# Four pieces of a weight load: cut across the columns instead of across the partitions

## The chip, the core and the metric

The kernel runs on one core of a Trainium2 chip. The metric is device time in microseconds (us): the median of three runs of the whole program, one launch. The core has five engines with a program each: TensorE (PE, matrix products, with its weight loads as PEld), VectorE (DVE), ScalarE (ACT), GpSimd (POOL) and SyncE (SP). Transfers between the chip's main memory (HBM) and the core's memory (SBUF, 128 partitions) are issued by SP, ACT or POOL and carried out by 16 DMA engines. A transfer is taken apart into packets, here one for each contiguous run of bytes, a row of a partition.

## What is computed

Attention with 4 batches, 12 heads, 448 positions and 64 channels, whose heads are mixed before and after the softmax, and behind it a gated feed-forward layer:

```python
scores = scale * np.matmul(q, k.transpose(0, 1, 3, 2))
scores = np.einsum('bhij,hg->bgij', scores, w_pre)
attn = np.exp(scores - np.max(scores, axis=-1, keepdims=True))
attn = attn / (np.sum(attn, axis=-1, keepdims=True) + 1e-09)
attn = np.einsum('bhij,hg->bgij', attn, w_post)
x = np.matmul(attn, v)                # to (1792, 768)
gate = 1.0 / (1.0 + np.exp(-(x @ w_gate)))
out = (gate * (x @ w_val)) @ w_out    # 768 -> 1536 -> 768
```

## The kernel before

**The attention** runs to about 350 us of the profile. The queries of a batch are cut into blocks of up to 120, a block into sets of ten, and two sets make a unit; there are 92 units. The main loop has a slot for each unit and does in slot s the parts of several units: `regroup` of unit s+5, `premix` and `rowmax` of unit s+2, `expo` of the same, `norm`, `scale` and `p_lo` of unit s+1, `postmix` and `mix` of unit s, and parts of the scores of a coming block and of the weighted sum `av` of the last one.

The scores lie in SBUF tiles named st with the queries on the partitions. Mixing heads needs them with heads and queries on the partitions, so `regroup` (L206; L208 for a lone set) moves them with two transfers a unit from st into one of four tiles T, 120 rows of 1792 bytes each, from SBUF to SBUF. `premix` (L216) reads T with eight matmuls. T is issued in slot s for slot s+3 where `premix` reads it. Its buffer is one of four, and becomes free with the `premix` of four units earlier.

**The queue around the change.** SP issues nearly every transfer of this part, in program order: the T of each slot, k of the next batch (L137, 128 rows of 1792 bytes), v (L171, 128 rows of 4096 bytes), q (L145), the stores xs of the attention's result (L274, rows of up to 480 bytes), and the pieces of the weights that this change touches (L1005).

**The weights.** They come as 64-bit floats and are turned into 32-bit ones on the chip. A weight tile has 128 partitions and 768 numbers, so 6144 bytes a partition. It is read from the fourth byte on (`[:, 3:]`), 6141 bytes a row, so that the words come to lie as the conversion wants them. Most tiles are loaded with one transfer of 128 rows (L1035, after the attention). The first eight are taken during the attention by `early(k, step)`, tile k from slot 6+7k on: steps 0 to 3 in slots 0, 1, 2 and 3 of the tile load a piece each (L1005); step 4, in slot 8, is POOL's first pass (`top`, L1041), which reads one byte of each of the 768 words of all partitions; further passes of POOL follow in slots 9 and 10; steps 7 and 8 (slots 11 and 12) convert half of the columns each on DVE (L1059); steps 9 and 10 take the sums of the two halves on ACT (L981); step 11 (slot 14) stores the tile (L1063). Three buffers named raws are used in turn.

The order of the instructions on every engine is that of the program; no scheduler moves them. The feed-forward layer behind the attention follows a plan that is made before the launch from costs and due times; the change touches none of them.

Of the kernel before, what the change touches and what calls it, by code (L numbers as in the profile page):

```python
# [15 lines left out]
I8 = mybir.dt.int8  # L16
# [452 lines left out]
class _Moe:  # L469
# [530 lines left out]
    def early(self, k, step):  # L1000

        raw = self.free["R"][k % len(self.free["R"])]
        if step < 4:
            rows = slice(32 * step, 32 * step + 32)
            self.nc.sync.dma_start(out=raw.bitcast(I8)[rows, :8 * self.WE - 3], in_=self.src[k].bitcast(I8)[rows, 3:])  # L1005
            return
        names = ("raw", k), ("half", k)
        self.at.update({names[0]: raw, names[1]: self.free["H"][0]})
        if step < 7:
            self.top(k, step - 4, self.nc.gpsimd)  # L1010
        elif step < 9:
            self.convert(names[0], k, step - 7)
        elif step < 11:
            self.sum_of(names[0], ("w", k // 4), k % 4, step - 9, self.at[names[1]].bitcast(F16))
        else:
            self.keep_w(names[0], k, self.nc.sync)
        for name in names:
            del self.at[name]
# [241 lines left out]
```

## Time and profile before

| | |
|---|---|
| median of 3 runs | 824.03 us (817.82 to 831.54) |
| the profiled execution | 823.65 us, of which the span of the trace is 821.8 us |
| busy: PE, DVE, ACT, POOL | 778.4, 648.9, 550.8, 276.5 us |
| weight pieces (L1005) | 32 transfers, 191.9 KB each |
| transfers into T (L206, L208) | 176 of 210.0 KB, 8 of 105.0 KB |

A busy engine in such a profile is not an engine at its peak: the ends of pipelined matmuls are modelled. The chain is read backwards from the end of the program or of a stretch: at each step it names what released the step that came last. The DMA share of a stretch is the mean busy share of the 16 DMA engines. q1 is the queue of SP's and ACT's transfers. A packet of a few bytes stands at the end of each engine's part of a transfer.

### The profile page before, as it was taken

What the parts mean: (1) busy time and instruction counts of PE and PEld (TensorE: products, weight loads), DVE (VectorE), ACT (ScalarE), POOL (GpSimd) and SP (SyncE); (2) the same over time, 40 slices, a digit from 0 to 9 for tenths busy, and PEclk for the clock granted to TensorE, in tenths of its full rate; (3) what the DMA queues carried; (4) which work ended last, traced back from release to release, by engine and by line L of the source; (5) the groups of instructions that cost most, each with busy time, mean ns of one, the idle gap of its engine ahead of it and who ended that gap; (6) DMA issues with size and microseconds to landing.
All of it is one profiled execution on the core that took longest, in us unless ns stands there. A gap on an engine that the chain in (4) does not pass through costs nothing.

```text
span 821.8 us, 23240 instructions
## 1 busy us (share of the span) xinstructions
PE 778.4 (95%) x9530; PEld 424.1 (52%) x9530; DVE 648.9 (79%) x1105; ACT 550.8 (67%) x1058; POOL 276.5 (34%) x438
## 2 busy tenths in 40 slices
PE   8889998999999999978999999999997999999998
PEld 2445555564644655654555555555553455455554
DVE  4979998898978989988998989679772998998000
ACT  3867887787767887868776867668762785653100
POOL 1535666555654644420122232224220312110000
PEclk9999999999999999979999999999999999999999
DMA  5787568868886575694725554755568789996001
GB/s 187 224 212 228 174 214 238 237 196 179 225 253 201 178 219 166 221 167 149 243 91 146 171 205 188 250 192 198 189 201 140 266 304 262 409 350 274 34 34 67
DMA packets 78690, 166.13 MB, mean 202 GB/s; under 512 B 20984, under 2 KB 54104, under 8 KB 78584
## 3 DMA queue, kind: packets, MB, share of 16 engines
q1 hardware_dynamic: 70920, 136.03, 55.3%
q0 software_dynamic: 7088, 28.13, 9.1%
q8 instruction: 74, 1.21, 0.6%
q10 hardware_dynamic: 576, 0.51, 0.2%
q14 instruction: 32, 0.26, 0.1%
HBM read 87.77 MB, written 38.15 MB: 153 GB/s over the span
## 4 chain that ended last, share of the span: by engine, by line
PE 63%; DMA 17%; ACT 6%; DVE 6%; issue 4%; POOL 2%; SPq 0%; ACTq 0%; POOLq 0%; DVEq 0%
PE bank L1114 27%; PE bank L1125 14%; PE pm L216 6%; PE av L285 6%; DMA T<-st 6%; PE qk L158 5%; PE mx L258 4%; DMA xs<-xt 3%; ACT e L228 3%; DMA k<-in_kp_dram 2%; DVE m L1098 2%; DVE nm L221 2%; DMA max_out<-one_out 2%; DMA m<-max_out 1%; ACT mix L266 1%
## 5 line engine op out<-in xcount | busy, mean ns | idle before, releaser
L1114 PEld LDWEIGHTS <-m 128*128 128x128 f16 x1512 | 148.3, 98 | 151.5 <-issue 10.9
L1114 PE MATMUL bank<-m,m 128*128 128x448 f16 x1116 | 216.1, 354 | 10.2 <-DVE m L1141 5.7
L228 ACT ACTIVATE e<-pm,nm 128x448 f32<-128x448 f32 x180 | 114.9, 639 | 66.2 <-DVE nm L221 58.9
L240 POOL TENSOR_SCALAR ph<-e,ss 128x448 f16<-128x448 f32 x180 | 112.7, 638 | 57.7 <-DVE ss L234 36.7
L221 DVE TENSOR_REDUCE nm<-pm 128x1 f32<-128x448 f32 x180 | 103.5, 615 | 30.4 <-PE pm L216 29.3
L246 DVE SCALAR_TENSOR_TENSOR pl<-e,ss,ph 128x448 f16<-128x448 f32 x180 | 121.8, 716 | 1.2 <-POOL ph L240 1.2
L1125 PEld LDWEIGHTS <-m 128*128 128x128 f16 x756 | 73.9, 98 | 69.9 <-DMA m<-w 1.1
L216 PE MATMUL pm<-T,w 64*64 64x448 f32 (+1 forms) x720 | 103.9, 567 | 2.9 <-DMA T<-st 2.2
L258 PEld LDWEIGHTS <-ph 64*128 64x128 f16 x2880 | 69.0, 95 | 71.6 <-issue 39.6
L266 ACT ACTIVATE mix<-mx 128x960 f32<-128x960 f32 (+1 forms) x92 | 102.8, 1117 | 4.0 <-PE mx L258 3.9
L285 PE MATMUL av<-mix,v 128*64 128x120 f32 (+1 forms) x1504 | 95.5, 271 | 9.9 <-issue 7.6
L158 PE MATMUL qk<-k,q 64*64 64x448 f32 (+2 forms) x640 | 98.4, 555 | 2.7 <-ACT st L164 2.7
L1125 PE MATMUL bank<-m,m 128*128 128x448 f16 x468 | 93.1, 352 | 0.6 <-DMA m<-w 0.6
L285 PEld LDWEIGHTS av<-mix,v 128*64 128x64 f32 x1504 | 75.3, 139 | 17.8 <-issue 10.6
L258 PE MATMUL mx<-w2hi,ph 64*128 64x60 f16 x1440 | 72.6, 190 | 9.0 <-ACT mix L266 8.4
L1114 PE MATMUL bank<-m 128*128 128x448 f16 x396 | 79.1, 356 | 0.0
L1049 POOL CAST raws<-raws 128x768 f16<-128x768 bf16 x36 | 37.6, 1045 | 122.7 <-ACT raws L1043 122.6
L258 PE MATMUL mx<-w2lo,ph 64*128 64x60 f16 x1440 | 72.3, 189 | 1.7 <-issue 1.7
L258 PE MATMUL mx<-w2hi,pl 64*128 64x60 f16 x1440 | 72.3, 189 | 0.0
L233 POOL TENSOR_SCALAR ss<-ss 128x2 f32<-128x2 f32 (+1 forms) x92 | 31.2, 339 | 118.7 <-ACT e L228 117.5
L1141 DVE TENSOR_TENSOR m<-bank,m 128x448 f32<-128x448 f32 x72 | 44.6, 620 | 24.5 <-PE bank L1114 16.7
L258 PEld LDWEIGHTS <-pl 64*128 64x128 f16 x1440 | 63.0, 95 | 0.0
(119 smaller groups left out, 1064.7 us busy)
## 6 DMA issues: line engine op xcount, KB each, us to landing
T<-st SPq DMA_DIRECT2D x176, 210.0 KB
m<-w SPq DMA_DIRECT2D x60, 384.0 KB
raws<-in_w_dram SPq DMA_DIRECT2D x28, 767.6 KB
hs<-m POOLq DMA_DIRECT2D x48, 224.0 KB, 4.8
m<-hs SPq DMA_DIRECT2D x15, 672.0 KB
w<-m POOLq DMA_DIRECT2D x21, 384.0 KB, 4.8
v<-in_vb_dram SPq DMA_DIRECT2D x12, 512.0 KB
raws<-in_w_dram SPq DMA_DIRECT2D x32, 191.9 KB
```

What stands on the lines that cost most here:

```text
L158: nc.tensor.matmul(sc[e][s0:s1, :S], lhsT=q[rows, c, s0:s1], rhs=k[rows, :], start=True, stop=True)
L216: nc.tensor.matmul(pm[bank][64 * x:64 * x + 64, :S], lhsT=w1[rows], rhs=T[rows, x], start=True, stop=True)
L221: nc.vector.tensor_reduce(nm[:, i:i + 1], pm[bank][:, :S], axis=AX.X, op=ALU.max, negate=True)
L228: nc.scalar.activation(out=e_t[u][:, i], in_=pm[units[u][2][i]][:, :S], func=AF.Exp, bias=nm_t[u][:, i:i + 1], scale=1.0, accum_out=ss_t[u ...
L240: nc.gpsimd.tensor_scalar(ph[:, i], e_t[u][:, i], ss_t[u][:, i:i + 1], 1.0, op0=ALU.mult, op1=ALU.mult)
L246: nc.vector.scalar_tensor_tensor(pl[:, i], e_t[u][:, i], ss_t[u][:, i:i + 1], p_t[u][0][:, i], op0=ALU.mult, op1=ALU.subtract)
L258: nc.tensor.matmul(mx[:, x, i, jb * HK:(jb + 1) * HK], lhsT=p[rows, i, JB[jb]:JB[jb] + 128], rhs=w[rows], start=(k == 0), stop=(k == 2))
L266: nc.scalar.activation(out=out.rearrange("p g (y r) -> p y g r", r=HALF), in_=mx_t.pop(u), func=AF.Copy, scale=1.0 / (P_UP * W_UP))
L285: nc.tensor.matmul(av_t[bi][64 * i:64 * i + 64, c % 4, :n], lhsT=vt[b, u][:, h + i, jb, :], rhs=mixes[bi % 2][:, jb, 2 * c + i, :n], start ...
L1114: self.nc.tensor.matmul(self.f32(bank), lhsT=w[a][:, k], rhs=x[b][:, k], start=self.START[i] and k == r == 0, stop=k == self.KH - 1 and r ...
L1125: self.nc.tensor.matmul(self.f32(bank), lhsT=w[a][:, k], rhs=b[bb], start=self.START[i] and j == k == r == 0, stop=j == OUT_TILES - 1 and ...
L1141: self.nc.vector.tensor_tensor(self.f32(out), self.f32(bank), self.f32(snap), op=ALU.add)
```

## The change

Each tile is still loaded in four pieces, in the same slots and by the same engine. A piece was a quarter of the partitions (32 rows, 6141 bytes each). It is now a quarter of the columns: 128 rows of 1536 bytes, in the last piece 1533. `self.WE` is 768, and `2 * self.WE` bytes are 192 of the 64-bit numbers.

```diff
         raw = self.free["R"][k % len(self.free["R"])]
         if step < 4:
-            rows = slice(32 * step, 32 * step + 32)
-            self.nc.sync.dma_start(out=raw.bitcast(I8)[rows, :8 * self.WE - 3], in_=self.src[k].bitcast(I8)[rows, 3:])
+            b, e = 2 * self.WE * step, min(2 * self.WE * (step + 1), 8 * self.WE - 3)
+            self.nc.sync.dma_start(out=raw.bitcast(I8)[:, b:e], in_=self.src[k].bitcast(I8)[:, b + 3:e + 3])
             return
```

On SP, the first tile's pieces stand like this between the transfers of k, q and T (T_170 to T_173 are the four T buffers; in brackets the semaphores that an instruction waits for):

```order
 L137 DMA k<-in_kp_dram 128x448 [waits DMAHW1_49]
-L1005 DMA raws<-in_w_dram 32x6141 [waits DMAHW2_49]
+L1005 DMA raws<-in_w_dram 128x1536 [waits DMAHW2_49]
 L206 DMA T_170<-st 120x1x448 [waits DMAHW3_49,DVE_49,Activation_49]
 L206 DMA T_170<-st 120x1x448 [waits DMAHW4_49,PE_49]
 L137 DMA k<-in_kp_dram 128x448 [waits DMAHW5_49]
-L1005 DMA raws<-in_w_dram 32x6141 [waits DMAHW6_49]
+L1005 DMA raws<-in_w_dram 128x1536 [waits DMAHW6_49]
 L206 DMA T_171<-st 120x1x448 [waits DMAHW7_49,PE_49]
 L206 DMA T_171<-st 120x1x448 [waits DMAHW0_49,PE_49]
```

No row has moved, and the pieces wait for the same semaphores; only their shape differs.

On DVE, in the middle of the attention, the first of a tile's two half-width conversions (L1059) stands among the work of a slot:

```order
 L164 COPY st<-qk 120x448 [waits PE_49]
 L246 SCALAR_TENSOR_TENSOR pl<-e,ss,ph 128x448 [waits Pool_49] x2
-L1059 SCALAR_TENSOR_TENSOR raws<-raws 128x384 [waits DMAHW7_49,DMAHW6_49,DMAHW2_49]
+L1059 SCALAR_TENSOR_TENSOR raws<-raws 128x384 [waits DMAHW6_49,DMAHW2_49]
 L234 RECIPROCAL ss<-ss 128x2 [waits Pool_49]
 L221 TENSOR_REDUCE nm<-pm_116 128x1 [waits PE_49]
```

It keeps its place and names the pieces that hold its own half of the columns, where it named pieces of all partitions; with some tiles the second conversion and ACT's sums (L981) name the rest.

## Rows read from the trace of the kernel before

**Rows 1.** The profile's page, part 4: the chain's shares by engine.
```profile
PE 63%; DMA 17%; ACT 6%; DVE 6%; issue 4%; POOL 2%; SPq 0%; ACTq 0%; POOLq 0%; DVEq 0%
```

**Rows 2.** The chain of 40 to 256 us: shares, then start, length and what.
```profile
by line: DMA T<-st 20.1%; PE pm L216 13.5%; PE av L285 13.2%; PE qk L158 9.2%; DMA xs<-xt 8.6%; PE mx L258 8.4%; DMA k<-in_kp_dram 5.0%; ACT e L228 3.7%; issue 3.5%; DVE nm L221 2.8%; ACT mix L266 2.1%; DVE pl L246 2.0%; ACT st L164 1.8%; P
...
52.16 8.87 DMA T<-st
...
219.19 9.07 DMA T<-st
228.33 7.67 DMA T<-st
...
245.40 7.35 DMA T<-st
```

**Rows 3.** The chain of 255 to 346 us: its shares.
```profile
by line: PE pm L216 22.4%; PE av L285 22.3%; PE mx L258 18.3%; PE qk L158 17.1%; ACT e L228 4.4%; ACT mix L266 3.4%; DMA T<-st 3.2%; issue 2.7%; DVE nm L221 2.6%; DVE pl L246 1.4%; ACT st L164 0.5%; DVE one_w L994 0.4%; DVE vm L176 0.4%; DV
```

**Rows 4.** Stretches, L216 alone: us, PE, PEld, clock, DMA share, GB/s.
```profile
43.00:65.00 22.00, 5.50 (x40) 1.04 (x40) 0.92 0.85 212
215.00:240.00 25.00, 8.81 (x46) 2.18 (x44) 1.00 0.88 228
255.00:280.00 25.00, 6.97 (x56) 1.54 (x60) 1.00 0.60 196
```

**Rows 5.** Instructions of the tiles raws: ns min/median/max, first and last start.
```profile
L1005 SPq DMA_DIRECT2D raws<-in_w_dram x32: 322/494/1441, 43.2 to 251.3; - x32
L1035 SPq DMA_DIRECT2D raws<-in_w_dram x28: 327/328/1026, 384.4 to 585.6; - x28
...
L1041 POOL TENSOR_SCALAR raws<-raws x16: 2172/2204/2223, 76.9 to 275.6; 128x768 int16<-128x768 int8 x8, 128x768 int32<-128x768 int16 x8
```

**Rows 6.** Who waited for L1005: engine, tile, line, us and times.
```profile
  PEld pm L216: 0.3, 2
```

**Rows 7.** SP's timeline in two places: start, length, line, transfer, count.
```profile
110.58 0.50 SPq L1005 DMA_DIRECT2D raws<-in_w_dram  x1
111.19 3.40 SPq L206 DMA_DIRECT2D T<-st  x4
114.69 0.45 SPq L171 DMA_DIRECT2D v<-in_vb_dram  x1
115.24 1.67 SPq L206 DMA_DIRECT2D T<-st  x2
...
220.01 0.50 SPq L1005 DMA_DIRECT2D raws<-in_w_dram  x1
...
238.89 0.33 SPq L1005 DMA_DIRECT2D raws<-in_w_dram  x1
```

**Rows 8.** Transfers of 554.5 to 556.5 us: packets, then q1's packets, MB, share.
```profile
DMA packets 149, 0.82 MB, mean 408 GB/s; under 512 B 16, under 2 KB 16, under 8 KB 149
...
q1 hardware_dynamic: 149, 0.82, 98.6%
```

**Rows 9.** The same of 87.8 to 89.4 us.
```profile
DMA packets 86, 0.25 MB, mean 153 GB/s; under 512 B 22, under 2 KB 56, under 8 KB 86
...
q1 hardware_dynamic: 86, 0.25, 53.6%
```

**Rows 10.** The same of 335 to 337 us.
```profile
DMA packets 301, 0.49 MB, mean 245 GB/s; under 512 B 28, under 2 KB 301, under 8 KB 301
...
q1 hardware_dynamic: 301, 0.49, 64.5%
```

**Rows 11.** The same of 84 to 86 us.
```profile
DMA packets 515, 0.24 MB, mean 121 GB/s; under 512 B 515, under 2 KB 515, under 8 KB 515
...
q1 hardware_dynamic: 515, 0.24, 41.7%
```

**Rows 12.** The same of 233.5 to 235.5 us.
```profile
DMA packets 282, 0.46 MB, mean 232 GB/s; under 512 B 23, under 2 KB 282, under 8 KB 282
...
q1 hardware_dynamic: 282, 0.46, 82.1%
```

## The prediction

> **What bounds the kernel now.** I read four views, from the whole to the single transfer. The chain of the whole program first [rows 1]: TensorE holds 63% of it and transfers 17%, so a transfer can set the time, if it is in the right stretch. The 32 pieces are issued between 43.2 and 251.3 us [rows 5], so only that stretch can answer directly. The chain of 40 to 256 us [rows 2] is quite another than that of 255 to 346 us [rows 3], where the same attention runs without pieces. In the first, transfers into T hold 20.1%, xs 8.6% and k 5.0%, together 33.7% of 216 us, or 73 us; in the second, T holds 3.2%. The legs are long: a T that is issued at 219.19 us releases its reader only after 9.07 us.
>
> The stretches [rows 4] say the same. In 215 to 240 us TensorE does 46 matmuls of L216 in 25 us; at eight to a slot that is 5.75 slots, 4.35 us each. In 255 to 280 us it is 56, or 3.57 us. The busy share of the 16 DMA engines is 0.88 in the slow stretch and 0.60 in the fast one, with the granted clock at 1.00 in both. So in part of the stretch the DMA engines are the bound, and what a piece costs them counts there. Elsewhere a piece is beside the path.
>
> **What a piece's own reader sees.** The four pieces of a tile are issued in slots 0 to 3 and POOL first reads the tile in slot 8; the first piece goes out at 43.2 us and the first L1041 runs at 76.9 us [rows 5]. The last piece has five slots, over 17 us at 3.57 us a slot, and the longest transfer leg of the chain that stands here is 9.07 us [rows 2]. Nobody waits for a piece but a weight load of L216, 0.3 us in two waits [rows 6]. The new form keeps that: POOL's first pass reads a byte of every word in all columns and needs all four pieces, as before. The waits that the change puts on the half-width DVE conversions and ACT sums name pieces that landed before POOL's pass began, so they cost nothing. If that cover went, POOL's pass would wait for a landing, and the tile's store behind it.
>
> **What the change adds and removes, step by step.** SP issues the same 32 instructions in the same places. Each goes from 32 rows of 6141 bytes to 128 rows of 1536 (1533 in the last of four), so the bytes are the same.
>
> *Issue on SP: 0.* A 32-row piece takes 494 ns in the median, 322 at the least; a whole tile with 128 rows (L1035) takes 328, 327 at the least [rows 5]. What follows is no slower behind many rows: two T take 1.67 us behind the 128 rows of v at 114.69 us, and four take 3.40 us behind a 32-row piece at 110.58 us, so 0.84 and 0.85 us each [rows 7].
>
> *Time on the DMA engines.* I work in rows, with the busy share times 16 engines times the window, over the rows in it. A piece has 32 rows, 32 pieces have 1024: 64 per engine, if they spread evenly.
> - An old row, cheapest: 554.5 to 556.5 us holds next to nothing but rows of a whole tile, same length, all 128 partitions: 98.6% of 32 engine-us over 133 rows, less the 16 small packets, is 236 ns [rows 8].
> - An old row as a piece: 87.8 to 89.4 us holds 30 long rows, 34 of T (86 packets, 22 under 512 bytes, 56 under 2 KB) and 22 small ones. 53.6% of 25.6 engine-us is 13.72; less 34 at 75 ns and 22 at no more than 26 ns leaves 10.6, or 353 ns [rows 9]. So a row costs half as much again when all 16 engines write into 32 partitions.
> - A new row is not in the trace. A row of 1792 bytes takes 75 ns where T is alone (64.5% of 32 us over 273) [rows 10], one of 480 takes 26 (41.7% of 32 us over 515) [rows 11]; on the line between them 1536 bytes take 65. Beside k loads, in the slow stretch, a row of 1792 takes 100 (82.1% of 32 us over 259, less the small ones) [rows 12]; by its length a new row would take 86.
> - So four new rows take 260 (alone), 344 (by length, beside others) or 400 ns (each as dear as the 1792) against 236 to 353. I set 344 against 353: both are prices of a busy stretch, and the piece is of the old form. The difference is -9 ns per old row; the ends are 260-353 = -93 and 400-236 = +164 ns.
>
> *What of it is on the path.* I counted in SP's order: 13 of the 32 pieces are issued inside a transfer leg of the chain or up to 2.5 us ahead of one; two rows per engine each. That is 26 rows: -0.2 us, with ends of -2.4 and +4.3. With all 64 rows on the path it is -0.6, with ends of -6.0 and +10.5.
>
> The sum: 823.65 us for the profiled execution, -0.2, is 823.45 us; I say 823.5. The median of the runs is 824.03, from 817.82 to 831.54, so this one is a usual one, and the runs scatter more than the sum moves.
>
> [...] The old piece shows 353 ns for a row that costs 236 over all partitions [rows 8, 9]. [...] The new row starts 3 bytes past its grid in HBM as the old one did, but four times as often. [...]
>
> **The rivals.**
> *Faster, the old pieces held up T.* Long rows that meet in 32 partitions keep their engines and the T rows behind them. For it: legs of 7 to 9 us in the stretch with pieces and 3.2% after it [rows 2, 3], and 353 against 236 ns. The chain has 20.1% of 216 us, 43 us, in T. Half of that excess gone would be about 18 us, 805 to 806. A more modest form, a fifth of T's legs gone, is 8.7 us: 815. Against it: the leg that starts at 228.33 us lasts 7.67 us, and SP issues no piece between 220.01 and 238.89 us [rows 2, 7]. What fills the engines there is k, and the slow slots go on without a piece.
>
> *Slower, four rows for one fill engines that are full.* This is one mechanism: at a DMA share of 0.88, each new row at 100 ns against an old one at 236 delays the T behind it, all 64 rows count, and 10.5 us makes 834. It decides where T, issued three slots before its use, lands later than that use; in the slow stretch that point is reached already [rows 2, 4]. Past 2% it would take 16.5 us, so 257 ns more per old row, a new row at 123 ns or over from 236, dearer than any 1792 row read here. [...] Against it: the old pieces already cost 353.
>
> *The change moves bytes that are hidden anyway.* Where no transfer is on the chain (19 pieces), nothing changes. This is the same result as the forecast, by another way: 823.65.
>
> **How the numbers follow.** The forecast with the hidden rival, a move of under 2.4 us down or 4.3 up: 0.66, and 823.5. Faster by 3 to 16 us by the T legs: 0.14; by more: 0.06. Slower by 5 to 16 us: 0.10; by more: 0.04. The range takes the bounds of all 64 rows, 823.65-6.0 and +10.5, hence 817.7 to 834.2; at the low end I go on to 815 for the fifth of T's legs, and the scatter of the runs (817.82 to 831.54) lies inside: 815 to 834. The forecast's own range is 821 to 828. Two per cent, 16.5 us, is about what a measurement of this kernel can tell from no change. Faster by more than that 0.06, within it 0.90, slower by more 0.04.
>
> **What would show it right or wrong.** Right: L1005 with 32 issues near 0.33 to 0.5 us; about 3,000 more packets on q1, most of 1536 bytes, at the same bytes; T still near a fifth of the chain of 40 to 256 us; the slots of 215 to 240 us still over 4 us. The row price is wrong if a stretch with pieces shows a DMA share that is 0.03 higher or lower at the same work. The cover is wrong if anyone on POOL, DVE or ACT waits for raws<-in_w_dram. The forecast is wrong if T's share of that chain falls under a tenth (then the first rival), or if waits of L216 for T rise by several us in stretches that had none, 65 to 115 us above all (then the second).

## The result and the profile after

The changed kernel takes 814.07 us in the median against 823.88 us of the kernel before, 20 runs of each, so 9.8 us less. Without the slow runs of either kernel the ratio is 0.9907, with a 95% interval of 0.9879 to 0.9934; it is that of the two means, which lie 7.7 us apart. The move is under 2%, but clear of the scatter, and 8 to 10 us by either measure. The forecast of 823.5 us, with a range of its own of 821 to 828, was wrong. The median lies 0.9 us under the low end of the wide range; 824.03 us times the ratio, 816.4 us, lies just inside it.

The profiled execution took 810.96 us (span 809.2), 3.1 us less than the median: the two traces differ by 12.7 us, the kernels by less. The chain of the whole program after the change, by engine, against [rows 1]:

```profile
PE 73%; DMA 9%; ACT 7%; DVE 6%; issue 2%; POOL 2%; SPq 0%; ACTq 0%; DVEq 0%; POOLq 0%
```

Transfers fell from 17% to 9%. All of it happened beside the attention. The last matmul of L216 stands at 356.5 us in the trace before and at 344.0 us in the one after (first the line of before, then that of after, from the list of instructions that read T, whose columns are ns min/median/max, first and last start):

```profile
L216 PE MATMUL pm<-T,w x720: 533/587/951, 17.4 to 356.5; 64*64 64x448 f32 x176, 60*64 60x448 f32 x4
...
L216 PE MATMUL pm<-T,w x720: 533/536/587, 16.6 to 344.0; 64*64 64x448 f32 x175, 60*64 60x448 f32 x5
```

That is 12.5 of the 12.7 us between the two profiled executions. Of these, 1.7 us stand already at the first piece (43.2 us before, 41.5 after), where nothing differs yet. The chain of 40 to 256 us after the change, as in [rows 2] (shares by line, then start, length and what):

```profile
by line: PE av L285 18.0%; PE pm L216 17.4%; PE qk L158 13.5%; PE mx L258 12.0%; DMA T<-st 8.2%; DMA xs<-xt 5.5%; ACT e L228 4.8%; ACT mix L266 3.1%; DVE nm L221 2.9%; issue 2.8%; POOL raws L1041 2.7%; ACT st L164 2.2%; DVE pl L246 2.1%; PO
...
189.71 7.71 DMA T<-st
218.42 8.71 DMA T<-st
```

T fell from 20.1% to 8.2% of it. The leg between two loads of k, with no piece ahead of it, is still there: 7.67 us at 228.33 before, 8.71 at 218.42 after. Those of 8.87, 9.07 and 7.35 us at 52, 219 and 245 us, all near a piece, are gone, and with them the longest T of the chain before, which [rows 2] leave out, 10.46 us at 135.92; a new one of 7.71 stands at 189.71 us.

The stretches of [rows 4] show the same by slots (us, PE, PEld, clock, DMA share, GB/s, of L216 alone; the first line is of before, the others of after):

```profile
115.00:140.00 25.00, 5.89 (x48) 1.25 (x48) 0.93 0.82 232
...
43.00:65.00 22.00, 6.01 (x52) 1.36 (x56) 1.00 0.87 245
115.00:140.00 25.00, 6.61 (x56) 1.25 (x48) 1.00 0.77 236
215.00:240.00 25.00, 8.91 (x48) 1.97 (x48) 1.00 0.88 250
```

43 to 65 us has 52 matmuls where there were 40, and moves 245 GB/s where it moved 212, at much the same busy share (0.87 and 0.85). 115 to 140 us has 56 where there were 48. In 215 to 240 us little has changed: 48 against 46.

What the DMA engines did is best read over the same work, from the first piece to 10 us past the last. The first two rows are of the kernel before, 43.2 to 261.3 us, the others of the changed one, 41.5 to 249.9 us (packets, then q1's packets, MB and share of 16 engines):

```profile
DMA packets 29267, 47.02 MB, mean 216 GB/s; under 512 B 9766, under 2 KB 25301, under 8 KB 29221
...
q1 hardware_dynamic: 29221, 46.35, 76.2%
```

```profile
DMA packets 32336, 47.07 MB, mean 226 GB/s; under 512 B 9766, under 2 KB 29373, under 8 KB 32289
...
q1 hardware_dynamic: 32289, 46.40, 75.3%
```

The bytes are the same and the packets 3068 more, but 76.2% of 218.1 us is 166.2 us on each engine, and 75.3% of 208.4 us is 156.9: 9.3 us less. Taken packet by packet from the same stretches of the two traces, it is not the pieces that became cheaper:

| packets of q1 | mean ns before | after | us on each engine before | after |
|---|---|---|---|---|
| the pieces (per old row: 1 long, then 4 short) | 349 | 4 x 91.2 = 365 | 22.3 | 23.3 |
| 1792 bytes (T and k) | 97.4 | 92.5 | 93.0 | 88.1 |
| 4 bytes (the end of a transfer on an engine) | 24.4 | 10.4 | 4.2 | 1.8 |
| 2880 bytes (q) | 180.2 | 163.7 | 11.3 | 10.3 |
| 4096 bytes (v) | 255.6 | 231.4 | 13.8 | 12.9 |

The pieces cost 1.0 us more; everything else costs some 10 us less. The rows of 1792 bytes that were in flight together with a row of a piece took 104.5 ns in the mean before and 94.0 after; the others took 93.0 and 91.4. So most of what they gained was gained beside a piece. The 4-byte packets are another matter, of which the last section tells.

### The profile page after: what moved, and what is told of

It is laid out like the page before. It is cut to its first block, busy times and chain, and to the rows that moved or that the text cites. A ratio compares the mean times of both kernels' runs of the same rounds, so it can differ in the third digit from the quotient of the medians.

```text
span 809.2 us, 23239 instructions
## 1 busy us (share of the span) xinstructions
PE 770.3 (95%) x9530; PEld 419.5 (52%) x9530; DVE 649.6 (80%) x1105; ACT 550.5 (68%) x1058; POOL 276.3 (34%) x438
## 4 chain that ended last, share of the span: by engine, by line
PE 73%; DMA 9%; ACT 7%; DVE 6%; issue 2%; POOL 2%; SPq 0%; ACTq 0%; DVEq 0%; POOLq 0%
PE bank L1114 29%; PE bank L1125 18%; PE av L285 7%; PE pm L216 7%; PE qk L158 6%; PE mx L258 5%; ACT e L228 3%; DMA T<-st 3%; DMA xs<-xt 2%; DVE nm L221 2%; DMA max_out<-one_out 2%; DVE m L1098 1%; ACT mix L266 1%; DMA m<-max_out 1%; DMA max_x<-vr 1%
## 5 line engine op out<-in xcount | busy, mean ns | idle before, releaser
L258 PEld LDWEIGHTS <-ph 64*128 64x128 f16 x2880 | 66.8, 93 | 70.8 <-issue 37.8
L216 PE MATMUL pm<-T,w 64*64 64x448 f32 (+1 forms) x720 | 100.2, 561 | 2.1 <-DMA T<-st 1.4
L158 PE MATMUL qk<-k,q 64*64 64x448 f32 (+2 forms) x640 | 95.6, 545 | 3.9 <-ACT st L164 3.9
L285 PE MATMUL av<-mix,v 128*64 128x120 f32 (+1 forms) x1504 | 93.3, 268 | 5.2 <-ACT xt L293 3.4
L258 PE MATMUL mx<-w2hi,ph 64*128 64x60 f16 x1440 | 70.6, 188 | 10.5 <-ACT mix L266 9.1
L285 PEld LDWEIGHTS av<-mix,v 128*64 128x64 f32 x1504 | 73.9, 138 | 12.5 <-ACT xt L293 4.3
L258 PE MATMUL mx<-w2lo,ph 64*128 64x60 f16 x1440 | 70.3, 187 | 1.2 <-issue 1.2
L258 PE MATMUL mx<-w2hi,pl 64*128 64x60 f16 x1440 | 70.3, 187 | 0.0
L233 POOL TENSOR_SCALAR ss<-ss 128x2 f32<-128x2 f32 (+1 forms) x92 | 30.0, 326 | 105.6 <-ACT e L228 104.3
L258 PEld LDWEIGHTS <-pl 64*128 64x128 f16 x1440 | 61.3, 93 | 0.0
```

What stands on the lines that cost most here:

```text
L158: nc.tensor.matmul(sc[e][s0:s1, :S], lhsT=q[rows, c, s0:s1], rhs=k[rows, :], start=True, stop=True)
L216: nc.tensor.matmul(pm[bank][64 * x:64 * x + 64, :S], lhsT=w1[rows], rhs=T[rows, x], start=True, stop=True)
L258: nc.tensor.matmul(mx[:, x, i, jb * HK:(jb + 1) * HK], lhsT=p[rows, i, JB[jb]:JB[jb] + 128], rhs=w[rows], start=(k == 0), stop=(k == 2))
L285: nc.tensor.matmul(av_t[bi][64 * i:64 * i + 64, c % 4, :n], lhsT=vt[b, u][:, h + i, jb, :], rhs=mixes[bi % 2][:, jb, 2 * c + i, :n], start ...
```

## The experiments

Two theories at first. **P**: what matters is which partitions a piece writes. **R**: what matters is how long its rows are, because short ones let other rows in between. Each ratio below is to runs of the kernel before on the same chip.

### Which partitions, or which length

The two parts of the change, one at a time: 32 rows of 6141 bytes in every fourth partition, and 32 neighbouring partitions with rows of 1533 bytes.

```diff
-            rows = slice(32 * step, 32 * step + 32)
+            rows = slice(step, 128, 4)
```

> A piece keeps its 32 rows of 6141 bytes, but takes every fourth partition instead of 32 neighbours. Theory P (which partitions a piece writes decides: rows that land in 32 neighbouring partitions collide with each other and hold the other transfers' rows behind them) expects what the changed kernel gives, a ratio of about 0.99 to the kernel before (some 814 us) and long rows near 240 to 290 ns in the mean instead of 349. Theory R (the length of a row decides: short rows let T's rows and TensorE's instruction loads in between) expects no change, 1.00 (824 us), and T's rows as dear as before (mean 91 ns).

Measured: 1.0512 (1.0466 to 1.0558), 865.42 us. Neither theory had that.

```diff
+            rows, n = slice(32 * step, 32 * step + 32), 2 * self.WE
+            out, src = (t.bitcast(I8)[rows].rearrange("p (c n) -> p c n", n=n) for t in (raw, self.src[k]))
+            self.nc.sync.dma_start(out=out[:, :, :n - 3], in_=src[:, :, 3:])
```

> A piece keeps its 32 neighbouring partitions, but each partition's row is cut into four rows of 1533 bytes (three bytes between them that nothing reads are left out). Theory P expects no gain, 1.00 (824 us) or a little above, since there are 98,000 more bytes' worth of row starts on crowded partitions, and rows well over 95 ns in the mean. Theory R expects the changed kernel's gain, 0.99 (814 us).

Measured: 0.9991 (0.9965 to 1.0018), 821.79 us. (The 98,000 bytes in that text are a slip: it is 3072 more rows.) Rows as short as the changed kernel's, in the old partitions, gain nothing. R falls. The mean of the short rows is 96.3 ns in the trace, near the changed kernel's 91.2, and the rows of 1792 bytes stay at 98.8 (104.8 beside a piece).

The two with 64 partitions and half the columns, neighbours and every second one:

```diff
+            rows, b = slice(64 * (step // 2), 64 * (step // 2) + 64), 4 * self.WE * (step % 2)
+            e = min(b + 4 * self.WE, 8 * self.WE - 3)
+            self.nc.sync.dma_start(out=raw.bitcast(I8)[rows, b:e], in_=self.src[k].bitcast(I8)[rows, b + 3:e + 3])
```

> A piece has 64 neighbouring partitions (0 to 63 or 64 to 127) and half the columns, rows of 3072 bytes. [...] Theory R expects half of the gain, 0.995, and the same as for every second partition.

Measured: 0.9985 (0.9955 to 1.0015), 821.39 us. Twice the partitions and half the row length give nothing that can be measured.

The other takes `rows = slice(step // 2, 128, 2)`, with the rest as in the last diff.

> As the kernel with 64 neighbouring partitions and rows of 3072 bytes, but a piece takes every second partition, so 64 partitions over the whole range. Theory P expects the whole gain, 0.99 (814 us). Theory R expects 0.995, and no difference to the 64 neighbouring partitions.

Measured: 1.0478 (1.0443 to 1.0513), 862.99 us.

Why both strided ones are slow, the waits of SP's own queue show, in 40 to 256 us of the first of them (engine, line, waited for, us, times, longest):

```profile
SPq L1005 <- POOL ss L233: 40.4, 15, 5.8
SPq L1005 <- DMA w<-raws: 21.4, 5, 5.7
```

There is no such row before. The three buffers lie side by side in one tile. It looks as if a slice with a stride over the partitions is taken as a range that reaches over the other buffers too: a piece waits for POOL and for the store of another tile, and every T behind it on SP waits as well. With these waits in them, the two runs say nothing of partitions.

### The same without those waits

The buffers as tiles of their own, first for the strided pieces, then for the pieces before, as a control:

```diff
-        raws = top.tile([128, 13 * H * D // 2], F32, name="raws")
+        raws = [top.tile([128, n * H * D // 2], F32, name=f"raws{i}") for i, n in enumerate((4, 4, 4, 1))]
...
```

> Every fourth partition again, 32 rows of 6141 bytes, but with the three buffers as tiles of their own, so that a piece does not wait for POOL's passes over a tile in another buffer (SP's waits are then those of the kernel before). [...] If striding itself is dear, it stays slow, 1.03 to 1.05. If only the number of partitions of a piece counts, 1.00.

Measured: 0.9902 (0.9866 to 0.9938), 814.23 us.

> The control for that: the kernel before, pieces of 32 neighbouring partitions, with the three buffers as tiles of their own. All theories expect 1.00 (0.997 to 1.003); what it differs by is to be taken off the strided one.

Measured: 0.9977 (0.9944 to 1.0010), 820.79 us. So the old long rows, 32 to a piece, give the changed kernel's time if the 32 partitions lie apart: 6.6 us between the two medians, with no overlap of the intervals. The length of a row and the number of partitions are the same in both. That the 5% of every fourth partition were the waits is shown as well: no piece waits for POOL any more. Every second partition was not tried again. The price of a long row that theory P named for every fourth partition, 240 to 290 ns, was missed: it is 337 in the mean, against 359 in the control. It is again the others that gained more, the rows of 1792 bytes beside a piece with 95.2 ns against 107.3.

### Which 64 partitions, or too few of them

The pair that tells these apart, with `slice(32, 96)` here and `slice(0, 64)` in the other:

```diff
+            to = self.free["R"][(k + step // 2) % len(self.free["R"])]
+            rows, b = slice(32, 32 + 64), 4 * self.WE * (step % 2)
+            e = min(b + 4 * self.WE, 8 * self.WE - 3)
+            self.nc.sync.dma_start(out=to.bitcast(I8)[rows, b:e], in_=self.src[k].bitcast(I8)[rows, b + 3:e + 3])
...
+        nc.gpsimd.memset(raws, 0.0)
```

Both kernels leave out half of each tile, which stays zero, so that they move as many bytes as the kernel before.

> A pair with the next kernel, alike but for the partitions. Every piece writes rows of 3072 bytes into partitions 32 to 95, the first two of a tile into its own buffer, the other two into the buffer of the next tile (which overwrites them), so the bytes stay those of the kernel before, but half of each tile is never loaded (zeros, from one memset of POOL at the start). [...] Theory N (only the number of partitions of a piece counts, and 64 are still too few) expects what 64 neighbours gave before, 0.9985, and the same in both kernels.

Measured: 0.9887 (0.9837 to 0.9938), 812.80 us.

> The other of the pair: partitions 0 to 63 in every piece, all else as in the one with 32 to 95, and half of each tile never loaded as there. [...] Number of partitions: equal to its pair.

Measured: 1.0002 (0.9968 to 1.0036), 822.36 us. The two differ in one number and by 9.6 us: the whole gain. Neither the length of a row, nor the count of partitions, nor a stride is different. So theory N, with equal times for the pair, falls. What in the path of a transfer sets 0 to 63 apart from 32 to 95, no trace here shows. The traces do speak against one reading, that pieces of 0 to 63 are carried by fewer DMA engines: both kernels wrote 2729 packets of 4 bytes, one for each engine's part of a transfer, in the stretches below. The transfers over the same work, of the kernel with 0 to 63 (43.3 to 262.0 us) and then of the one with 32 to 95 (41.6 to 248.7 us):

```profile
DMA packets 30364, 47.20 MB, mean 216 GB/s; under 512 B 9769, under 2 KB 25349, under 8 KB 30317
...
q1 hardware_dynamic: 30317, 46.53, 77.5%
```

```profile
DMA packets 30331, 47.17 MB, mean 228 GB/s; under 512 B 9769, under 2 KB 25298, under 8 KB 30284
...
q1 hardware_dynamic: 30284, 46.50, 74.9%
```

The same bytes take 169.5 us of each engine (77.5% of 218.7) and 155.1 us (74.9% of 207.1). Worked out in the same way from their traces, each from its first piece to 10 us past the last, the kernels whose pieces keep their four slots and bring no new waits fall into two groups, and the times go with them:

| pieces | us on each engine | ratio |
|---|---|---|
| 32 neighbours, long rows (before) | 166.2 | 1 |
| 32 neighbours, tiles of their own | 167.0 | 0.9977 |
| 32 neighbours, short rows | 165.8 | 0.9991 |
| 64 neighbours, halves | 168.3 | 0.9985 |
| 0 to 63 | 169.5 | 1.0002 |
| 32 to 95 | 155.1 | 0.9887 |
| every fourth, long rows, tiles of their own | 157.1 | 0.9902 |
| all 128, short rows (the change) | 156.9 | 0.9907 |
| all 128, short rows, tiles of their own | 157.3 | 0.9870 |

### How finely to cut

All over the 128 partitions: a tile in one transfer in slot 0, in two in slots 0 and 2, and in eight of 768 bytes a row in slots 0 to 7 (the last as an edit of the changed kernel).

```diff
+            if step == 0:
+                self.nc.sync.dma_start(out=raw.bitcast(I8)[:, :8 * self.WE - 3], in_=self.src[k].bitcast(I8)[:, 3:])
             return
```

> Each tile in one transfer of 128 rows of 6141 bytes, in slot 0; nothing in slots 1 to 3. If only the partitions that a transfer covers matter, the gain stays, 0.99, perhaps 0.985, since 24 transfers fewer are issued and a long row is cheaper by the byte (236 ns against four times 65). If the cutting into pieces also matters (a whole tile is 8 rows of 236 ns ahead of the next T on each engine, near 2 us), T comes late in that slot: 0.995 to 1.00.

Measured: 0.9927 (0.9889 to 0.9964), 816.09 us.

```diff
+            if step % 2 == 0:
+                b, e = 2 * self.WE * step, min(2 * self.WE * (step + 2), 8 * self.WE - 3)
```

> Each tile in two transfers over all partitions, 128 rows of 3072 bytes, in slots 0 and 2. Partitions alone: 0.99. Cutting matters: between the four pieces (0.99) and the whole tile.

Measured: 0.9931 (0.9899 to 0.9963), 817.69 us. One, two or four transfers cannot be told apart.

```diff
+            j = step if step >= 0 else 3 - step
+            b, e = self.WE * j, min(self.WE * (j + 1), 8 * self.WE - 3)
...
+        for step in range(-4, 0):
+            at(6 + 7 * k + 3 - step, moe.early, k, step)
```

> Each tile in eight transfers over all partitions, 128 rows of 768 bytes, in slots 0 to 7. Row starts are then 8 per old row; a row of 768 bytes costs some 37 ns alone (on the line between 480 and 1792 bytes), so 298 ns per old row against 260 for four, 2.4 us more over all on each engine, and 32 more transfers on SP at 0.33 to 0.5 us. Partitions alone: 0.99 to 0.995. If finer pieces let more through: under 0.99.

Measured: 1.0220 (1.0161 to 1.0278), 838.77 us, against all that was expected. T does not come later: the weight loads of L216 wait 0.9 us for it in 40 to 260 us, 8.2 before. But the eighth piece goes out in slot 7 and POOL reads the tile in slot 8. DVE's wait behind POOL and POOL's own, in 40 to 260 us (`top` is L1044 in this kernel, `norm` L233; the last line is of the kernel before):

```profile
DVE ss L234 <- POOL ss L233: 31.7, 13, 7.0
...
POOL raws L1044 <- DMA xs<-xt: 11.9, 3, 5.7
POOL raws L1044 <- DMA T<-st: 11.7, 2, 5.9
...
DVE ss L234 <- POOL ss L233: 5.3, 9, 1.2
```

Before, POOL's pass waited for no transfer. The profile names a piece for 2.4 us of the pass's waits, and xs and T for the rest; that these too are waits for the late piece is likely, since the pass reads neither, and not shown. `norm` stands behind `top` on POOL, and the softmax waits for `norm`. That run took the cover away that the prediction had put at five slots, and it costs more than the change gave. Eight pieces that end in time were not tried.

### Both together

> The changed kernel (four pieces over all partitions, rows of 1536 bytes) with the three buffers as tiles of their own. [...] If short rows cost anything that counts, it is slower than the strided pieces by 2 us or more.

Measured: 0.9870 (0.9832 to 0.9909), 813.94 us, beside 823.86 us before on that chip. It is level with the changed kernel's 0.9907 and with the strided 0.9902, within their intervals. Nothing here beats the changed kernel by a margin that can be measured.

## Why the prediction was wrong, step by step

**The bound: right.** Transfers set the time in part of the stretch, and the gain came in that part.

**The reader's slack: right.** The longest transfer leg of the chain was 10.79 us (a k at 41.31 us), not 9.07, still well under 17. After the change only weight loads of L216 wait for a piece (0.5 us, three times), as before, and the row of L1005 has the same median, 496 ns against the 494 of [rows 5]:

```profile
L1005 SPq DMA_DIRECT2D raws<-in_w_dram x32: 328/496/1462, 41.5 to 239.9; - x32
...
  PEld pm L216: 0.5, 3
```

The kernel with eight pieces, where one slot of slack is left, took 2.2% longer.

**The price of a row: right.** A piece's row was set at 353 ns from [rows 9]; all 1024 have 349 in the mean. A new row alone was put at 65 by the line between two lengths. In 106.4 to 107.2 us of the trace after, nearly nothing but new rows runs (116 of 1533 bytes, and nine of T), and it says so:

```profile
DMA packets 151, 0.19 MB, mean 243 GB/s; under 512 B 26, under 2 KB 151, under 8 KB 151
...
q1 hardware_dynamic: 151, 0.19, 67.9%
```

67.9% of 12.8 engine-us over 125 rows is 69.5 ns with the 26 small packets in it, and 64 if those are taken at 26 ns. In the busy stretch four rows cost 365 where 344 were set. So the term is +1.0 us for all 64 old rows of an engine instead of -0.6: a small miss. In 41.5 to 249.9 us of the trace after, the 3072 rows of 1536 bytes and the 1024 of 1533 both take 65 ns in the median and 62 at the least.

**What of it is on the path: the step that failed.** It counted the pieces' own rows and nothing else: 13 of 32 pieces, -0.2 us. The pieces' own time hardly moved, and that part of the sum holds. What moved is the time of the rows that run beside them, which had no term: they gained some 10 us of each engine over the same work, less the pieces' 1.0 us, and the median fell by 9.8 us. The prediction also read the 353 ns of an old row in a piece, against 236 in a whole tile [rows 8, 9], as the price of 32 partitions. Most of that gap is the busy stretch: over every fourth partition the same rows still cost 337, and 359 in the control. What the partitions of a piece decide is in the main what its neighbours pay: 104.5 ns before and 94.0 after for a row of 1792 bytes beside a piece. Why they pay it, no trace here shows.

**The rivals.** The first one, in its modest form, comes nearest to what happened: rows that meet in 32 partitions hold T, a fifth of T's legs, 815 us, at a chance of 0.14. The argument against it was the leg at 228.33 us, with no piece ahead of it [rows 2, 7]. It was true and remains so: that leg is still there after the change, with 8.71 us. But it spoke of one leg. The gain came where pieces run: 43 to 65 us went from 40 to 52 matmuls of L216, and 115 to 140 us from 48 to 56. The mark that was named for this rival, T under a tenth of the chain, is met with 8.2%, but it is a poor mark: the kernel with partitions 0 to 63, which gained nothing, has 8.5% in the same stretch. The time of the DMA engines over the same work tells the kernels apart, and the share of T in one chain does not. The length of the rows, which this rival named beside the partitions, has no part in the gain.

**The clock.** 43 to 65 us was granted 0.92 before and 1.00 after, and the whole execution 0.983 and 0.991. 8% of 22 us is 1.8 us, so up to that much may be in the 12.7 us between the two traces, and as much in 115 to 140 us, granted 0.93 before and 1.00 after; both are estimates from these clocks. But the clock is not the cause of the gain: the profiled executions of the old pieces in tiles of their own and of partitions 0 to 63 had 0.989 and 0.990, at 821.73 and 818.46 us, and neither kernel gained.

## What to carry to other kernels

Ask which partitions a transfer touches before asking how long its rows are: 64 partitions in the middle gave the whole gain (0.9887), 64 at the bottom none (1.0002). Cut a large load along its columns, so that every piece covers all partitions (0.9907 here). And price a transfer also by what it does to those beside it: where the DMA engines are near full (0.85 to 0.88 here), its own time can change by 1 us while the others' falls by ten. A slice with a stride over the partitions of a shared tile can bring waits that cost more than it saves (1.0512 and 1.0478 here), and pieces that go out one slot ahead of their reader went with a loss of 2.2%, more than the change gave.

## What the runs showed that was not expected

The packet of 4 bytes that ends a transfer on an engine took 24.4 ns in the mean before the change and 10.4 ns after it, with a median of 9 in both, though nothing of it was altered. That is 2.4 of the some 10 us, and it does not follow the partitions alone: it took 24.5 ns with the old pieces in tiles of their own, 16.4 with long rows in every fourth partition, but 11.2 with short rows in the old 32 partitions. That last kernel gained nothing (0.9991), so the shorter packets by themselves bought no time.

TensorE's waits that the profile puts down to nothing it shows ("issue") fell too: before the weight loads of L285 in 43 to 255 us, first in the kernel before and then after the change:

```profile
PEld av L285 <- issue: 9.2, 6, 3.3
...
PEld av L285 <- issue: 4.2, 5, 1.8
```

The kernel with partitions 0 to 63 has 9.2 us there and the one with 32 to 95 has 4.0. They do not go with the 4-byte packets: the short rows in the old partitions have 8.5 us. That these are instructions which arrive late by the same engines is a guess, from the transfers of 16 KB that the trace shows on the queue for instructions (35 in 43.2 to 261.3 us before); it was not tried.
